# Cosine attention and a highway layer: all short products in two row tiles of TensorE, on four PSUM tiles of two banks

## The chip, the cores and the metric

One NeuronCore of a Trainium2 chip runs the whole program. The time is that of one execution on the device in microseconds (us); a smaller number is better. Five engines have instruction streams of their own, each in order: TensorE (PE; its weight loads are shown as PEld), VectorE (DVE), ScalarE (ACT), GpSimd (POOL) and SyncE (SP, which here issues DMAs only). They wait for each other through semaphores.

## The reference

The inputs are q, k and v of 8 batches x 12 heads x 448 rows x 64, two 768 x 768 weights and a bias.

```python
q_n = q / (np.linalg.norm(q, axis=-1, keepdims=True) + 1e-06)
k_n = k / (np.linalg.norm(k, axis=-1, keepdims=True) + 1e-06)
scores = np.matmul(q_n, k_n.transpose(0, 1, 3, 2)) / tau
scores = scores - np.max(scores, axis=-1, keepdims=True)
attn = np.exp(scores)
attn = attn / (np.sum(attn, axis=-1, keepdims=True) + 1e-09)
attn_out = np.matmul(attn, v)
x = attn_out.transpose(0, 2, 1, 3).reshape(B * S, H * D)
H = np.maximum(x @ w_h, 0.0)
T = 1.0 / (1.0 + np.exp(-(x @ w_t + b_t)))
out = T * H + (1.0 - T) * x
```

## The kernel before

**Tiling.** Heads are worked in pairs: step s = 6 b + p is pair p of batch b, 48 steps in all. The two heads of a pair have 64 dimensions each, so a block of 128 partitions holds both. Of the 448 rows of a head, 384 are the main rows (three chunks of 128) and 64 the tail. A batch's output rows go through the highway layer in four groups i (g = 4 b + i): three of 128 x 768, and the 64 tail rows as the fourth, laid out as 128 x 384.

**One step.** `scaled` normalises q and k (L254). `turn` brings them to [dimension, row], by seven TensorE transposes of 128 x 128 and a copy (L577, L580, L257) in batches 0 to 3, and by a DMA in batches 4 to 7. `scores` multiplies three chunks of keys with all queries of both heads, each head in its row tile of 64 (L637, "qk"), and ACT takes the exponential (L643). The key tails of both heads come in one full-array product (L652, "qkt") with its own exponential (L656). `attend` multiplies the exponentials with v, which has a column of ones for the sums: three parts of seven matmuls (L685 with the key tails of both heads in one, L689) and one of eight for the query tails (L705), all full array with 65 moving columns, 130 in L685. DVE takes the reciprocal of the sums (L713) and writes x (L715).

**The highway layer.** `ffn` turns x, by TensorE in batches 0 and 7 (L757), else by DMA, and multiplies it with w_t and w_h (L793). These products run in two row tiles of 64 already. Two row tiles must not write one PSUM bank at once, so each tile takes one half of the columns in one bank; in part 1 they swap banks, after a wait for part 0 to end (L786). The group of tail rows uses two column tiles (L777). ACT takes tanh (L816, L817), DVE the rectified product and the gate (L830, L835, L838), DVE or POOL the last sum (L844), SP stores (L850, L854).

**PSUM.** Three tiles of two banks ("pS", ring S) hold the scores and the highway products; two tiles of one bank ("pB", ring B) hold turned blocks, tail scores and attention sums. A tail group's two products share one pS tile.

**Norms.** The inverse norms of batch 0 are exp(-0.5 ln(n)) on ACT; those of the others are seven DVE operations per group (L460 to L466). The Tanh table holds no Ln, so ACT loads tables twice in all.

**Order.** The program is first recorded as operations, each with its engine, then replayed in the order that the tuple `ORDER` gives; `SLOTS` gives the buffer of each new tile, `MOVED` the operations that go to the second of two possible engines, and `URGENT` which POOL operations DVE has to wait for. No scheduler changes that afterwards. The start, where POOL issues the first loads (L345, L371), is in the same list.

```python
    plan = pl.follow(ORDER, SLOTS)
```

Of the kernel before, what the change touches and what calls it, by code (L numbers as in the profile page):

```python
# [8 lines left out]
FP32 = mybir.dt.float32  # L9
# [161 lines left out]
def kernel(  # L171
# [11 lines left out]
    nc = tc.nc  # L183
# [4 lines left out]
    MH = DM // 2  # L188
    NCH = 3
    inv_tau = 1.0 / float(tau)  # L190
    BY_DMA = (4, 5, 6, 7)
    assert (B, NH, S, D) == (8, 12, 448, 64)

    sb = ctx.enter_context(tc.tile_pool(name="sb", bufs=1))
# [771 lines left out]
```

## Time and profile before

| | |
|---|---|
| median of 3 runs | 274.05 us (273.81 to 274.11) |
| profiled execution | 269.76 us, of which the span of instructions is 268.0 us |
| busy, share of the span | PE 91%, DVE 82%, ACT 77%, POOL 43% |
| granted TensorE clock, mean | 0.967 |
| mean rate of the DMAs | 161 GB/s |
| most time by group | ACT L643 exponentials, 144 x 924 ns; PE L793 highway products, 1152 x 323 ns |

A row of a group gives line, engine, operation, what it writes and reads, the count, then busy time in us and the mean of one in ns, then the engine's idle time before these operations and what ended it. A row of instructions in order of time begins with the start and the duration in us. Matmuls are pipelined: the duration of one holds its latency, and the next starts long before it ends, so that what a matmul costs is read from the starts. A row of stretches gives the busy time of each engine between two times, then the granted clock of TensorE, the share of the DMA engines and their rate.

### The profile page before, as it was taken

What the parts mean: (1) busy time and instruction counts of PE and PEld (TensorE: products, weight loads), DVE (VectorE), ACT (ScalarE), POOL (GpSimd) and SP (SyncE); (2) the same over time, 40 slices, a digit from 0 to 9 for tenths busy, and PEclk for the clock granted to TensorE, in tenths of its full rate; (3) what the DMA queues carried; (4) which work ended last, traced back from release to release, by engine and by line L of the source; (5) the groups of instructions that cost most, each with busy time, mean ns of one, the idle gap of its engine ahead of it and who ended that gap; (6) DMA issues with size and microseconds to landing.
All of it is one profiled execution on the core that took longest, in us unless ns stands there. A gap on an engine that the chain in (4) does not pass through costs nothing.

```text
span 268.0 us, 9080 instructions
## 1 busy us (share of the span) xinstructions
PE 243.8 (91%) x3783; PEld 164.3 (61%) x3783; DVE 220.0 (82%) x501; ACT 206.1 (77%) x279; POOL 116.2 (43%) x150
## 2 busy tenths in 40 slices
PE   6088987899999999999999998999999999999990
PEld 2043665667776667666766775766567757777650
DVE  6598999999999989997999988999877953556483
ACT  3378999789999989989788898969778897671210
POOL 8757359455554567335551535226132501141200
PEclk9567999999999999999999999999999999999996
DMA  7999999999969696999889999999757837123143
GB/s 131 210 192 183 178 199 210 196 183 193 149 97 224 145 172 65 192 213 199 206 136 155 186 244 162 193 137 224 173 115 214 134 63 177 59 92 120 32 181 101
DMA packets 103738, 43.14 MB, mean 161 GB/s; under 512 B 97552, under 2 KB 100624, under 8 KB 103696
## 3 DMA queue, kind: packets, MB, share of 16 engines
q0 software_dynamic: 38464, 16.32, 49.1%
q1 hardware_dynamic: 64000, 25.80, 47.4%
q8 instruction: 30, 0.49, 0.7%
q10 hardware_dynamic: 1232, 0.43, 0.7%
q14 instruction: 12, 0.10, 0.1%
HBM read 37.82 MB, written 11.01 MB: 182 GB/s over the span
## 4 chain that ended last, share of the span: by engine, by line
PE 64%; DVE 17%; DMA 8%; issue 4%; ACT 2%; POOL 2%; SPq 1%; DVEq 0%; POOLq 0%; ACTq 0%
PE pS L793 27%; PE pS L637 8%; PE pB L689 7%; PE pS L777 6%; DMA qT<-qn 6%; PE pB L652 4%; PE pB L705 3%; PE pB L685 3%; PE pB L577 3%; DMA qr<-in_q_dram 2%; DVE os L844 2%; DVE x L715 2%; DVE f L416 2%; PE pB L306 1%; DVE kb L254 1%
## 5 line engine op out<-in xcount | busy, mean ns | idle before, releaser
L643 ACT ACTIVATE E<-pS 128x896 f16<-128x896 f32 x144 | 127.4, 924 | 23.1 <-PE pS L637 21.9
L793 PEld LDWEIGHTS <-xT 64*128 64x128 f16 x1152 | 54.5, 94 | 31.2 <-issue 1.3
L793 PE MATMUL pS<-wh,xT 64*128 64x384 f16 x576 | 58.0, 323 | 0.0
L793 PE MATMUL pS<-wt,xT 64*128 64x384 f16 x576 | 57.1, 323 | 0.0
L637 PE MATMUL pS<-qT 64*128 64x384 f16 x288 | 43.5, 331 | 1.8 <-DMA qT<-qn 1.0
L689 PE MATMUL pB<-vp,E 128*128 128x65 f16 x864 | 43.3, 194 | 0.0
L830 DVE SCALAR_TENSOR_TENSOR hm<-pS,x 128x768 f16<-128x768 f32 (+1 forms) x33 | 27.3, 834 | 17.5 <-PE pS L793 6.9
L689 PEld LDWEIGHTS <-E 128*128 128x128 f16 x864 | 38.5, 98 | 0.7 <-issue 0.6
L637 PEld LDWEIGHTS <-qT 64*128 64x128 f16 x576 | 22.7, 95 | 19.5 <-issue 4.6
L254 POOL TENSOR_TENSOR qn<-kr,rs 128x384 f16<-128x384 f16 x24 | 19.8, 828 | 32.5 <-issue 10.0
L685 PE MATMUL pB<-vp,Et 128*128 128x130 f16 x144 | 31.9, 222 | 0.5 <-DVE vp L257 0.4
L844 POOL TENSOR_TENSOR os<-x,hm 128x768 f32<-128x768 f16 (+1 forms) x11 | 16.7, 1516 | 34.6 <-DVE hm L838 16.4
L817 ACT ACTIVATE tt<-pS 128x768 f16<-128x768 f32 x24 | 19.6, 821 | 14.4 <-PE pS L793 14.3
L715 DVE SCALAR_TENSOR_TENSOR x<-pB,rd 128x448 f16<-128x448 f32 x48 | 29.8, 622 | 1.1
L656 ACT ACTIVATE Et<-pB 128x512 f16<-128x512 f32 x48 | 29.1, 610 | 1.7 <-PE pB L652 1.5
L637 PE MATMUL pS<-tT,qT 64*128 64x64 f16 x282 | 27.6, 190 | 0.0
L705 PE MATMUL pB<-vp,E 128*128 128x65 f16 x288 | 18.4, 194 | 0.6 <-DVE x L715 0.6
L254 POOL TENSOR_TENSOR qn<-qr,rs 128x384 f16<-128x384 f16 x17 | 14.4, 853 | 9.0 <-DVE os L844 3.5
L844 DVE TENSOR_TENSOR os<-x,hm 128x768 f32<-128x768 f16 (+1 forms) x21 | 17.6, 836 | 0.2
L685 PEld LDWEIGHTS <-Et 128*128 128x128 f16 x144 | 14.0, 97 | 5.6 <-issue 4.1
L254 DVE TENSOR_TENSOR qn<-qr,rs 128x384 f16<-128x384 f16 x30 | 16.8, 566 | 0.5 <-POOL qn L254 0.4
L713 DVE RECIPROCAL rd<-pB 128x7 f32<-128x7 f32 x48 | 9.4, 199 | 8.4 <-PE pB L705 4.0
(110 smaller groups left out, 437.4 us busy)
## 6 DMA issues: line engine op xcount, KB each, us to landing
out_dram<-os SPq DMA_DIRECT2D x24, 384.0 KB, 3.2
vr<-in_v_dram POOLq DMA_DIRECT2D x8, 576.0 KB, 11.7
kr<-in_k_dram POOLq DMA_DIRECT2D x7, 576.0 KB, 9.9
qr<-in_q_dram POOLq DMA_DIRECT2D x7, 576.0 KB, 10.2
qt<-in_q_dram SPq DMA_DIRECT2D x16, 96.0 KB, 5.2
vt<-in_v_dram SPq DMA_DIRECT2D x16, 96.0 KB, 5.2
out_dram<-os SPq DMA_DIRECT2D x16, 96.0 KB, 2.3
kt<-in_k_dram SPq DMA_DIRECT2D x14, 96.0 KB, 6.0
```

What stands on the lines that cost most here:

```text
L254: return (nc.vector if eng == "DVE" else nc.gpsimd).tensor_mul(out_, a, c)
L637: ins = nc.tensor.matmul(dst, lhsT=qT[ln, 384 + 128 * c : 512 + 128 * c], rhs=rhs, start=True, stop=True)
L643: return nc.scalar.activation(R("E", s)[:, c, :, 0:448], R("S", 3 * s + c)[:, :, 0:448], AF.Exp, scale=inv_tau)
L656: op("ACT", f"expt {s}", lambda: nc.scalar.activation(R("Et", s)[:, 64:576], R("B", ("S", s))[:, :], AF.Exp, scale=inv_tau), key + 3, r=[( ...
L685: nc.tensor.matmul(U[:, 2 * c : 2 * c + 2, :].rearrange("p g e -> p (g e)"), lhsT=Et[:, 128 + 128 * c : 256 + 128 * c], rhs=vp[:, 6:8, :]. ...
L689: ins = nc.tensor.matmul(U[:, 2 * c + ab, :], lhsT=EF[:, j, 576 * ab + 128 * c : 576 * ab + 128 * c + 128], rhs=vp[:, 3 * ab + j, :], star ...
L705: ins = nc.tensor.matmul(U[:, 6, :], lhsT=lt, rhs=rh, start=(n == 0), stop=(n == 7))
L715: op("DVE", f"ev {s}", lambda: nc.vector.scalar_tensor_tensor(out=R("x", b)[:, :, D * p : D * p + D], in0=U_()[:, :, 0:D], scalar=0.0, in1 ...
L793: ins = nc.tensor.matmul(P[:, h, 0:MH], lhsT=lt, rhs=rh, start=(part == 0 and cc == (-1 if wi == 0 else 0)), stop=(part == 1 and cc == CC ...
L817: return nc.scalar.activation(T.rearrange("p (h m) -> p h m", h=2), P[:, :, 0:MH], AF.Tanh, scale=0.5)
L830: return nc.vector.scalar_tensor_tensor(out=o_, in0=i0, scalar=0.0, in1=xs, op0=ALU.max, op1=ALU.subtract)
L844: op(en, f"out{wd} {g}", lambda: eng.tensor_add(R("os", g)[:, 0:W], xall(), R("hm", g)[:, 0:W]), at + 0.1, r=[("gg", g), ("x", b)], w=[("o ...
```

## The change

Ring B goes; ring S has four tiles of two banks, and everything that TensorE writes goes through it. A tail group of the highway layer takes one tile for each of its products.

Everything that used the full array but the 20 pieces of filling work at the start (`warm`) is split over two row tiles of 64, which write two different banks. A turn of a block is two transposes of 64 columns side by side, whose result is put together again by the copy's access pattern. The tail scores become three parts: each row tile holds one head's keys and takes half of the queries per bank; the banks are swapped after the first part and swapped back for the third. They have an exponential for the main queries and one for the tails. The attention products become four parts of seven matmuls per row tile, 56 a pair in place of 29; each row tile sums over one half of the rows of v, first into the blocks of one bank, then, after a wait, into those of the other. v's tails get one row block per pair with zeros around it in place of two.

The inverse norms of batches 1 and 2 are taken by ACT too (`LOGS`), with the first tanh held until they are done. One square of batch 2 goes to ACT or POOL. The very last tail group takes its gate as (x + 0.5 h) + tanh x 0.5 h, so that only two DVE operations follow the tanh, and its two stores go out on SP and ACT.

`ORDER`, `SLOTS`, `MOVED` and `URGENT` are new. In the new order POOL issues the loads of the first rows of k and q ahead of the bias.

```diff
--- before.py
+++ after.py
...
     BY_DMA = (4, 5, 6, 7)
+    LOGS = 2
...
-              qT=3, tT=2, E=3, Et=3, rd=2, x=3, xT=2, tt=3, hm=3, os=4, S=3, B=2)
+              qT=3, tT=2, E=3, Et=3, rd=2, x=3, xT=2, tt=3, hm=3, os=4, S=4)
...
         S=ring("pS", NR["S"], [128, 2, 512], FP32, ps),
-        B=ring("pB", NR["B"], [128, 512], FP32, ps),
...
+    def half(r):
+
+        return slice(64 * r, 64 * r + 64)
+
+    def flat(i):
+        return R("S", i).rearrange("p k c -> p (k c)")
+
     def R16(i):
-        return R("B", i).bitcast(FP16)
-
-
+
+        return flat(i).bitcast(FP16).rearrange("p (k c) -> p k c", k=2)
+
+    def to_turn(T, at, block):
+
+        for r in range(2):
+            ins = nc.tensor.transpose(T[:, r, 64 * at : 64 * at + 64], block[half(r)], ident[half(r), half(r)])
+        return ins
+
+    def turned(T, lo, n):
+        return T[:, :, 64 * lo : 64 * (lo + n)].rearrange("p r (n l) -> p n r l", l=64)
+
+    def in_blocks(a):
+        return a.rearrange("p n (r l) -> p n r l", l=64)
...
-            eng = pick(eng, "DVE" if eng == "ACT" else "POOL" if b == 1 else "ACT")
+            eng = "ACT" if b == 2 and t else eng
+            eng = pick(eng, "POOL" if b in (1, 2) else "DVE" if eng == "ACT" else "ACT")
...
-        if name[0] == "0":
+        if int(name[0]) <= LOGS:
...
-                at = 128 * (c + 1 - z)
-                nc.tensor.transpose(T[:, at : at + 128],
-                                    R("qn", s // 2)[:, z, c // NCH, c % NCH].rearrange("l ab d -> l (ab d)"), ident[:, :])
+                to_turn(T, c + 1 - z, R("qn", s // 2)[:, z, c // NCH, c % NCH].rearrange("l ab d -> l (ab d)"))
...
             kt_ = kb0[:, :, :] if s == 0 else R("kb", b)[:, p]
-            return nc.tensor.transpose(T[:, 768 * z : 768 * z + 128], kt_.rearrange("l ab d -> l (ab d)"), ident[:, :])
-
-        op("PE", f"turn {s}", fn, key, mode="F",
-           r=[("qn", s // 2, s % 2), ("kb0", 0) if s == 0 else ("kb", b, 0), ("id", 0)], w=[("B", ("T", ti))])
+            return to_turn(T, 6 * z, kt_.rearrange("l ab d -> l (ab d)"))
+
+        op("PE", f"turn {s}", fn, key, mode="T",
+           r=[("qn", s // 2, s % 2), ("kb0", 0) if s == 0 else ("kb", b, 0), ("id", 0)], w=[("S", ("T", ti))])
...
+    swap = {}
+
+    def after(ins, on):
+        tc.add_manual_dep(ins.ins, on.ins.name, mybir.DependencyInfo(
+            mybir.DependencyClass.Sync, mybir.DependencyReason.SCHED_ONLY), reason="order of engines")
+
+    def swapped(name, part):
+
+        if part == 0:
+            return None
+        held = nc.tensor.nop()
+        after(held, swap[name])
+        return held
+
+    def hold(ins, held, r):
+        if held is not None:
+            after(ins, held)
+        return None if r else held
...
-        def ft():
-            S_ = R("B", ("S", s))
+        def ft(part):
+
+            S_ = R("S", ("Q", s))
             qT = R("qT", s // 2)[:, 1 + 6 * z : 4 + 6 * z].rearrange("p c l -> p (c l)")
             keys = R("tT", b)[:, p] if b in BY_DMA else R("qT", s // 2)[:, 13 * z]
-            for dst, rhs in ((S_[:, 0:64], tails()), (S_[:, 64:448], qT), (S_[:, 448:512], tails())):
-                ins = nc.tensor.matmul(dst, lhsT=keys, rhs=rhs, start=True, stop=True)
+            held = swapped(("Q", s), part)
+            for i in ((0,), (0, 1), (1,))[part]:
+                for r in range(2):
+                    h, ln = r ^ (part % 2), half(r)
+                    dst, rhs = ((S_[:, h, 32:224], qT[ln, 192 * h : 192 * h + 192]),
+                                (S_[:, h, 0:32], tails()[ln, 32 * h : 32 * h + 32]))[i]
+                    ins = nc.tensor.matmul(dst, lhsT=keys[ln], rhs=rhs, start=(part == i), stop=(part == i + 1))
+                    held = hold(ins, held, r)
+            swap["Q", s] = ins
             return ins
 
-        op("PE", f"qkt {s}", ft, key + 3, mode="F", r=tok, w=[("B", ("S", s))])
-        op("ACT", f"expt {s}", lambda: nc.scalar.activation(
-            R("Et", s)[:, 64:576], R("B", ("S", s))[:, :], AF.Exp, scale=inv_tau), key + 3,
-           r=[("B", ("S", s))], w=[("Et", s)])
+        for part in range(3):
+            op("PE", f"qkt {s} {part}", lambda part=part: ft(part), key + 3 + 0.1 * part, mode="T",
+               r=tok + [("Q0", s, n) for n in range(part)], w=[("S", ("Q", s))] + [("Q0", s, part)])
+
+        def et():
+
+            for at, lo, n in ((64, 0, 32), (192, 32, 192)):
+                ins = nc.scalar.activation(R("Et", s)[:, at : at + 2 * n].rearrange("p (h q) -> p h q", h=2),
+                                           R("S", ("Q", s))[:, :, lo : lo + n], AF.Exp, scale=inv_tau)
+            return ins
+
+        op("ACT", f"expt {s}", et, key + 3, r=[("S", ("Q", s))], w=[("Et", s)])
...
+        def terms(r, g):
+
+            ln, got = half(r), []
+            EF, Et = R("E", s).rearrange("l c ab q -> l c (ab q)"), R("Et", s)
+            abs_ = range(2) if g == 6 else (g % 2,)
+            if r in abs_:
+                q0 = 64 - 64 * r if g == 6 else 192 + 64 * (g - r)
+                got.append((g, Et[ln, q0 : q0 + 128], 6 * NP + 1 + 4 * p))
+            for ab in abs_:
                 for j in range(NCH):
+                    q0 = 384 + 64 * ab if g == 6 else 576 * ab + 64 * (g - ab)
+                    got.append((g, EF[ln, j, q0 : q0 + 128], 6 * p + 3 * ab + j))
+            return got
+
+        def part_of(n):
+
+
+            part, lot = n // 2, n % 2
+            held, U = swapped(("U", s), part) if lot == 0 else None, U_()
+            todo = [[x for g in (((0, 1), (2, 3)), ((5, 4), (6,)))[r ^ part][lot] for x in terms(r, g)] for r in range(2)]
+            assert len(todo[0]) == len(todo[1])
+            for k in range(len(todo[0])):
+                for r in range(2):
+                    g, lt, at = todo[r][k]
+                    dst, rhs = U[:, g, :], R("vp", b)[half(r), at, :]
+                    first = n == k == 0
+                    if first:
+                        w = slice(0, 4) if r == 0 else slice(4, 7)
+                        dst = U[:, w, :].rearrange("p g e -> p (g e)")
+                        rhs = R("vp", b)[half(r), at - r : at + (4, 2)[r], :].rearrange("l g e -> l (g e)")
+                    ins = nc.tensor.matmul(dst, lhsT=lt, rhs=rhs, start=first, stop=(n == 3 and k == len(todo[r]) - 1))
+                    held = hold(ins, held, r)
+            if n == 1:
+                swap["U", s] = ins
             return ins
...
-        for c in range(NCH):
-            op("PE", f"av {s} {c}", lambda c=c: full(c), key + 0.3 * c, mode="F", r=rd, w=[("B", ("U", s))])
-        op("PE", f"avt {s}", tail, key + 1, mode="F", r=rd, w=[("B", ("U", s))])
+        for n in range(4):
+            op("PE", f"av {s} {n}", lambda n=n: part_of(n), key + 0.3 * n, mode="T",
+               r=rd + [("U0", s, m) for m in range(n)], w=[("S", ("U", s)), ("U0", s, n)])
...
+        def finish_last():
+
+            k_ = key + 5
+            op("DVE", f"ac {g}", lambda: nc.vector.scalar_tensor_tensor(
+                out=R("os", g)[:, 0:W], in0=R("hm", g)[:, 0:W], scalar=0.5, in1=R("x", b)[:, 6, :], op0=ALU.mult, op1=ALU.add),
+               k_, r=[("hm", g), ("x", b)], w=[("ac", g)], u=[("hm", g), ("os", g)], port=True)
+            op("DVE", f"hh {g}", lambda: nc.vector.tensor_scalar_mul(R("hm", g)[:, 0:W], R("hm", g)[:, 0:W], 0.5),
+               k_, r=[("hm", g), ("ac", g)], w=[("hh", g)], u=[("hm", g)], port=True)
+            op("DVE", f"ggh {g}", lambda: nc.vector.tensor_mul(R("tt", g)[:, 0:W], R("tt", g)[:, 0:W], R("hm", g)[:, 0:W]),
+               k_, r=[("tt", g), ("hh", g)], w=[("gg", g)], u=[("tt", g), ("hm", g)], port=True)
+            op("DVE", f"outh {g}", lambda: nc.vector.tensor_add(R("os", g)[:, 0:W], R("os", g)[:, 0:W], R("tt", g)[:, 0:W]),
+               k_, r=[("gg", g), ("ac", g)], w=[("os", g)], u=[("tt", g)], port=True)
+            store_tails((("SP", nc.sync), ("ACT", nc.scalar)))
...
-                op("ACT", f"th{1 if tail else 2} {g}", tanh, at, r=[("Pd", g, 0)], w=[("tt", g)], u=[bank])
+                logs = [("rn", n, p) for n in range(LOGS + 1) for p in range(1 if n == 0 else 0, 7)] if g == 0 else []
+                op("ACT", f"th{1 if tail else 2} {g}", tanh, at, r=[("Pd", g, 0)] + logs, w=[("tt", g)], u=[bank])
```

More of the change, by code (lines that the diff above doesn't have):

```diff
@@ L670, in vtcast @@
     def vtcast(b, key):
-        for ab in range(2):
-            eng = pick("DVE", "POOL")
-            op(eng, f"vtc {b} {ab}", lambda ab=ab, eng=eng: copied(
-                eng, R("vp", b)[64 * ab : 64 * ab + 64, :, 6 + ab, 0:D], R("vt", b)[64 * ab : 64 * ab + 64, :, :]),
-               key, r=[("vt", b), ("zvp", min(b, 1))], w=[("vp", b, 6)], port=eng != "ACT")
+        eng = pick("DVE", "POOL")
+        op(eng, f"vtc {b}", lambda: copied(eng, v_tails(R("vp", b))[:, :, 0:D], R("vt", b)[:, :, :]),
+           key, r=[("vt", b), ("zvp", min(b, 1))], w=[("vp", b, 6)], port=eng != "ACT")
     def attend(b, p, key):
@@ L737, in ffn @@
         last_ = b == B - 1 and i == 2
+        last_tail = b == B - 1 and tail
         nb = 3 if tail else 6
@@ L794, in mm @@
                                                stop=(part == 1 and cc == CC - 1))
-                        if held is not None:
-                            after(ins, held)
-                            held = None if r else held
+                        held = hold(ins, held, r)
                 swap[g, wi] = ins
@@ L840, in ffn @@
            r=[("gt", g), ("hm", g)], w=[("gg", g)], u=[("tt", g), ("hm", g)], port=True)
-        last = b == B - 1 and i >= 2
-        en = "DVE" if last else pick("POOL", "DVE")
+        en = pick("POOL", "DVE")
         eng = nc.vector if en == "DVE" else nc.gpsimd
```

136 lines of the change are left out of this document (56 added, 80 removed), and 152 rows, old and new, of tables (MOVED, ORDER).

## The prediction

> **What bounds the kernel now.** I read the page's parts 1 and 2 first, then a table of stretches, then the instructions of TensorE in order of time, and at last the two ends of the chain of waits.
>
> ```profile
> PE 243.8 (91%) x3783; PEld 164.3 (61%) x3783; DVE 220.0 (82%) x501; ACT 206.1 (77%) x279; POOL 116.2 (43%) x150
> ```
>
> The stretches end where attention of batch 3 and of batch 6 is done (the 24th and the 42nd write of x at L715).
>
> ```profile
> core 0: us, PE busy (x) PEld busy (x) DVE busy (x) ACT busy (x) POOL busy (x), PEclk, DMA share, GB/s
> 0.00:30.00 30.00, 18.66 (x159) 9.98 (x159) 23.55 (x63) 18.48 (x28) 20.59 (x38) 0.77 1.33 180
> 30.00:130.50 100.50, 96.66 (x1615) 68.09 (x1613) 94.04 (x217) 94.13 (x126) 55.46 (x68) 1.00 1.16 174
> 130.50:217.90 87.40, 85.42 (x1382) 57.44 (x1378) 76.67 (x170) 71.82 (x99) 32.23 (x40) 1.00 0.99 169
> 217.90:268.00 50.10, 43.09 (x639) 28.78 (x635) 25.78 (x55) 21.66 (x29) 7.91 (x6) 0.96 0.37 110
> ```
>
> After the start TensorE is nearly always busy: 96.7 of 100.5 us, then 85.4 of 87.4. But in the first of these two stages DVE and ACT are also at 94%; in the second they have 11 and 16 us to spare. So less work for TensorE is worth its full size in the later stages and at most about 6 us in the first. And busy is not the same as at its peak, as its instructions show:
>
> ```profile
> 120.95 0.21 PE L637 MATMUL pS<-tT,qT 64*128 64x64 f16 x2
> 121.09 0.20 PE L652 MATMUL pB<-tT,qT 128*128 128x64 f16 x1
> ...
> 121.82 0.25 PE L705 MATMUL pB<-vp,E 128*128 128x65 f16 x3
> ...
> 122.07 0.22 PE L685 MATMUL pB<-vp,Et 128*128 128x130 f16 x1
> 122.13 0.35 PE L689 MATMUL pB<-vp,E 128*128 128x65 f16 x6
> 122.32 0.19 PE L652 MATMUL pB<-tT,qT 128*128 128x64 f16 x1
> 122.35 0.32 PE L652 MATMUL pB<-qT 128*128 128x384 f16 x1
> 122.51 0.19 PE L652 MATMUL pB<-tT,qT 128*128 128x64 f16 x1
> 122.64 0.34 PE L637 MATMUL pS<-qT 64*128 64x384 f16 x2
> 122.81 0.19 PE L637 MATMUL pS<-tT,qT 64*128 64x64 f16 x2
> 122.84 0.33 PE L637 MATMUL pS<-qT 64*128 64x384 f16 x2
> ```
>
> Count by starts, since a duration holds the latency too. A 64-column step costs 0.03 us, whether it is one full-array matmul (122.32 to 122.35) or two in row tiles (122.81 to 122.84). From the full array to row tiles (122.51 to 122.64) and back (120.95 to 121.09) the same step takes 0.13 and 0.14: a change of mode costs 0.10 us.
>
> **The change, part by part.** I cost the work by starts from these rows and count instructions along the order of each program.
>
> Modes. TensorE changes between full array, row tiles and column tiles 135 times before and 40 times after (56 of the 95 fewer lie in the stages up to batch 3, 29 in the next, 10 behind). 95 x 0.10 = -9.5 us.
>
> Turns. Seven 128-column turns take 0.40 us:
>
> ```profile
> 96.41 0.51 PE L577 MATMUL pB<-ident,qn 128*128 128x128 f16 x6
> 96.75 0.22 PE L580 MATMUL pB<-ident,kb 128*128 128x128 f16 x1
> 96.81 0.50 PE L577 MATMUL pB<-ident,qn 128*128 128x128 f16 x6
> ```
>
> that is 0.057 each. Afterwards a block is two 64-column turns side by side, one 64-column step, 0.03. 221 blocks x 0.028 = -6.2 us, nearly all before batch 4.
>
> Attention products. One part with the key tails takes 0.25 us (122.07 to 122.32), the query tails the same for eight (121.82 to 122.07), so a 65-column step is 0.032 and a pair 1.02 (three parts of 0.254, and 0.26). Afterwards there are 56 half-height matmuls in 28 pairs: 27 x 0.0325 and a first one of 260 columns, 0.11, together 0.99. That is -1.5 us over 48. It assumes that the two of a pair overlap as at 122.81; no row has a long run of short row-tile matmuls, so the ends are 0.03 and 0.065 (one behind the other) a step. I take the first, since the row is the same shape but one column. Scores of key tails: 0.22 before (122.32 to 122.51 and a step), and 0.08 + 0.08 + 2 x 0.03 after: nothing.
>
> The Trainium skill, "TensorEngine Tiling (Array Packing)", Performance Considerations, speaks against this part: each matmul has some 60 cycles of overhead, so one should not tile where a dimension is small already. By the 25 ns that "TensorE: Matmul & The Clock Gate", Back-to-back issue gap, gives for that, 56 matmuls would take an estimated 1.40 us and the sum would come out some 20 us higher. The pair at 122.81 starts its successor after 0.03 us, so this trace does not bear it out for row tiles.
>
> Swaps. Where the row tiles exchange banks, a wait (L786) holds the sequencer until the part before has ended. There are 144 new ones: two per pair in the tail scores, one in the products.
>
> ```profile
> L786 PEldq EVENT_SEMAPHORE  x48: 51/51/51, 48.7 to 256.8; - x48
> ```
>
> The 48 of before cost nothing, since at least 0.19 us of other work lies between. The price is the end of the last matmul (0.19 after its start for 65 columns, about 0.24 for 192), 0.05 for the wait, and by my estimate 0.05 before and 0.03 behind it, since the waits of before all had slack; less the step itself: 0.28 us, less the other work that the order puts between. In the new order 52 of the 144 have less than that, most of them 0.19 and ten of them none: together +6.9 us (4.8, 1.3 and 0.8 by stage).
>
> PSUM. Before, 200 uses shared three tiles of two banks and 153 two of one bank; after, 361 uses share four. Readers hold a tile as long as these rows say:
>
> ```profile
> L643 ACT ACTIVATE E<-pS 128x896 f16<-128x896 f32 x144 | 127.4, 924 | 23.1 <-PE pS L637 21.9
> L830 DVE SCALAR_TENSOR_TENSOR hm<-pS,x 128x768 f16<-128x768 f32 (+1 forms) x33 | 27.3, 834 | 17.5 <-PE pS L793 6.9
> L656 ACT ACTIVATE Et<-pB 128x512 f16<-128x512 f32 x48 | 29.1, 610 | 1.7 <-PE pB L652 1.5
> L715 DVE SCALAR_TENSOR_TENSOR x<-pB,rd 128x448 f16<-128x448 f32 x48 | 29.8, 622 | 1.1
> ```
>
> I laid TensorE's costs along each order and asked at every hand-over if the work between a tile's last matmul and its next first one covers 0.3 us and the reader. Past the first 20 us of TensorE's work, before falls short at 7 of 296, by 2.2 us in all; after at 71 of 298, by 19.0 us (11.9, 5.6, 1.5 by stage). One wait of TensorE pushes back the next use of all four tiles, so these do not add up: at the least a quarter, 4.8 us, at the most 19. I take the quarter, since the swaps' stalls help as well.
>
> So TensorE by stage: -11.5 + 4.8 + 3.0 = -3.7; -3.7 + 1.3 + 1.4 = -1.0; -1.8 + 0.8 + 0.4 = -0.6.
>
> ACT and DVE. The tail's exponential becomes two; from 0.610 for 512 columns and 0.494 for 384 (next fence) 64 columns take 0.2, so +0.08 each, +4 in all; three Ln/Exp pairs for batches 1 and 2, about 0.6 each, +1.8; in return three squares of 1.18 fewer, and one smaller one and two copies of q and k, some 0.9 each: ACT +0 to +1. DVE loses 21 Newton steps (L460 to L466, 0.2 to 0.26 each) and six half casts of v's tails (0.5), and takes on squares and products: some -5, about 2 of it in the second stretch. So that stretch can't go below 94 us of ACT; one slice of 20 us in it has ACT busy for 19.94, so at 97% it ends at 97, a gain of 3.5. I take -3.5 there in place of -3.7.
>
> ```profile
> L816 ACT ACTIVATE tt<-pS 128x384 f16<-128x384 f32 x8 | 4.0, 494 | 6.4 <-PE pS L777 4.1 <-DVE hm L830 2.3
> L260 ACT ACTIVATE sq<-kr 128x1152 f16<-128x1152 f16 x9 | 10.5, 1179 | 0.2 <-DMA qr<-in_q_dram 0.2
> L449 ACT ACTIVATE rs<-n,tiny 128x36 f32<-128x36 f32 x2 | 0.7, 338 | 0.8 <-DVE n L422 0.8
> 60.00:80.00 20.00, 19.87 (x350) 14.43 (x345) 18.86 (x38) 19.94 (x26) 11.08 (x13) 1.00 1.04 147
> ```
>
> Start. The first squares wait for q's rows, which POOL issues behind a bias load that waits for a clear:
>
> ```profile
> 4.90 0.52 POOL bth L371
> 5.42 0.73 POOL qr L345
> 6.15 5.67 DMA qr<-in_q_dram
> 11.90 0.85 ACT sq L260
> 12.78 0.76 DVE f L416
> ```
>
> The new order issues those four loads first: 2 to 3 us earlier. But the first pair's normalising now stands behind their folds (L416, 0.76) on DVE, and more loads are in flight at once. -1.5, between -3 and 0.
>
> End. The last tanh waits for DVE, which reads the same tile:
>
> ```profile
> 261.03 0.56 DVE L830 SCALAR_TENSOR_TENSOR hm<-pS,x 128x384 f16<-128x384 f32 x1 [0.39 <-PE pS L777]
> 261.50 0.95 DVE L844 TENSOR_TENSOR os<-x,hm 128x768 f32<-128x768 f16 x1
> 261.68 0.49 ACT L816 ACTIVATE tt<-pS 128x384 f16<-128x384 f32 x1 [2.02 <-DVE hm L830]
> 263.64 1.11 SPq L850 DMA_DIRECT2D out_dram<-os  x2
> ```
>
> Afterwards it is a tile of its own and the two stores go out on two queues: -1.0 and -0.5 at best; but DVE has the 0.95 of L844 and some 0.6 of new operations to do meanwhile. -0.7, between -0.2 and -1.2.
>
> Sum: -3.5 - 1.0 - 0.6 - 1.5 - 0.7 = -7.3. The profiled execution took 269.76 (span 268.0), so 262.4 for it; the median of the runs stands 4.3 higher, 274.05, and so comes to 266.7.
>
> **Rivals.** First, ACT and DVE decide up to batch 3: each waits for the other often enough that the stage gains 1 us and the start nothing. 274.05 - 1.0 - 1.6 - 0.7 = 270.7. For it: three engines at 94% or more; against: the slice where ACT is full.
>
> Second, slower: four PSUM tiles are too few, and each short hand-over is paid alone. With a share s of the 19 us paid, the change is -17.2 + 6.9 + 19 s - 2.2, so it loses from s = 0.66; at 0.85 it is +3.7, 278. For it: the cover was near 1 us at the median before and is 0.2 to 0.3 now; against: before, TensorE hardly waits for PSUM, and one wait serves four tiles.
>
> Third, slower as well: row-tile matmuls of 65 columns don't overlap in long runs. 56 x 0.0325 - 1.02 = 0.80 a pair, +38.5 in place of -1.5: about 305.
>
> Fourth, the change does not free TensorE at all, since other waits take up all it saves: 274.
>
> **How the numbers follow.** Forecast (262 to 269.5) 0.50; ACT and DVE 0.20; PSUM 0.17; no overlap 0.05; no change 0.03; better than 262, with no hand-over paid and the start at its best, 0.05. Within 0.2% is about what a measurement can't tell from no change. Faster: 0.50 + 0.20 + 0.05 = 0.75; same 0.03; slower 0.22. The range leaves out the fast end, no overlap and the worst of PSUM: 261.5 to 278; the forecast alone has 262 to 269.5.
>
> **What would show it.** Right: 65-column pairs starting every 0.033 us; few 0.10 us steps; new idle of TensorE of 5 to 12 us with ACT E and DVE x as releasers; the end of batch 3 at about 125.5, of batch 6 at 212. Wrong: pairs at 0.065; TensorE's gaps over 17 us; ACT busy under 90% in the first stage with TensorE waiting for it.

## The result and the profile after

The changed kernel takes 306.42 us (median of four runs, 302.94 to 308.92), the kernel before in the same session 273.93: a ratio of 1.1229, 95% interval 1.0962 to 1.1496. The forecast was 266.7. (Where runs of one kernel lie more than 1.5% above its fastest they count as slow: they are left out of ratios and intervals, but not of the medians given here.) The profiled execution took 305.67, span 303.9. From the page of the kernel after (part 1, queues, chain):

```profile
PE 249.1 (82%) x5541; PEld 173.0 (57%) x5541; DVE 215.6 (71%) x473; ACT 204.9 (67%) x328; POOL 118.4 (39%) x153
...
q8 instruction: 44, 0.72, 0.9%
...
PE 68%; issue 11%; DVE 9%; ACT 7%; DMA 3%; POOL 0%; ACTq 0%; PEldq 0%; DVEq 0%; POOLq 0%
```

and the queue's line before:

```profile
q8 instruction: 30, 0.49, 0.7%
```

TensorE's busy time hardly rose (243.8 before), but it fell from 91% of the span to 82%, and 11% of the chain is "issue": time in which the engine waited for nothing that the profile shows. The instructions went from 3,783 matmuls and as many weight loads to 5,541 of each, and the packets of queue 8 from 30 to 44, 16 KB each. The same stretches as before, of the kernel after (stage ends by the 24th and 42nd write of x):

```profile
0.00:30.00 30.00, 15.98 (x243) 8.94 (x243) 22.66 (x59) 17.80 (x30) 22.48 (x38) 1.00 1.30 177
30.00:154.90 124.90, 101.34 (x2498) 72.15 (x2496) 93.66 (x201) 93.87 (x149) 54.83 (x67) 0.93 0.95 144
154.90:252.90 98.00, 88.20 (x1948) 62.09 (x1946) 72.20 (x161) 70.10 (x114) 35.27 (x45) 0.97 0.91 147
252.90:303.90 51.00, 43.54 (x860) 29.80 (x856) 27.10 (x54) 23.08 (x38) 5.79 (x4) 0.99 0.41 111
```

By the start of its last write of x, batch 3 ends at 154.9 and not at 125.5, batch 6 at 252.9 and not at 212. In the second stretch no engine is full any more (TensorE 81%, ACT and DVE 75%), and TensorE's clock is 0.93. What TensorE waited for, in the view of waits:

```profile
PE pS L773 <- issue: 17.6, 12, 3.3
PE pS L334 <- DVE fill L305: 9.7, 1, 9.7
PE pS L874 <- issue: 7.3, 4, 3.2
PE pS L283 <- issue: 2.1, 2, 1.2
PE pS L682 <- ACT E L688: 1.4, 3, 0.7
PE pS L861 <- issue: 1.1, 1, 1.1
```

19 idle times of up to 3.3 us, 28.1 us together, are put down to "issue"; ACT's exponential and DVE's output of attention, which were to be the releasers, are far behind. (The 9.7 us of L334 are the filling work at the start, which waits for a clear.) One of the 19, in TensorE's instructions in order of time:

```profile
90.57 0.36 PE L773 MATMUL pS<-vp,E 64*128 64x65 f16 x12
90.76 0.25 PE L703 MATMUL pS<-qT 64*128 64x192 f16 x2
...
91.53 0.25 PE L773 MATMUL pS<-vp,E 64*128 64x65 f16 x5
95.05 0.23 PE L773 MATMUL pS<-vp,E 64*128 64x65 f16 x1 [3.26 <-issue]
95.17 0.21 PE L703 MATMUL pS<-tT,qT 64*128 64x32 f16 x2
95.22 0.48 PE L874 MATMUL pS<-bth,ones 64*128 64x384 f16 x2
95.50 1.17 PE L874 MATMUL pS<-wt,xT 64*128 64x384 f16 x6
96.45 0.53 PE L874 MATMUL pS<-bth,ones 64*128 64x384 f16 x2
```

TensorE stops in the middle of a run of products whose operands are all there. And this is where it stops: counting the rows of its stream from the first (matmuls, weight loads and the waits that its sequencer executes, 11,282 in all), these stops stand at number 705, 961, 1217, 1729 and so on, 256 rows or a multiple of it apart, and a packet of 256 instructions of 64 bytes has come in 1.2 to 1.7 us before it goes on. For this one the transfers from 92.5 to 94.0 us show the packet, among loads and stores:

```profile
q1 hardware_dynamic: 997, 0.29, 88.6%
q0 software_dynamic: 185, 0.07, 37.4%
q8 instruction: 1, 0.02, 3.9%
```

It came from 92.85 to 93.79. So TensorE had run out of instructions. Counted by starts, 20 of the 42 block boundaries behind 30 us have such a stall, 32.6 us in all; in the kernel before none has. And the long ones cost once more, since the clock (the number behind POOL's count) falls to half; 95.50 to 96.45 above holds three pairs of matmuls, 0.32 each in place of 0.16. Behind 30 us the trace has seven such stretches of 3.4 us at 0.50: after all six stalls of 2 us and more and after one of 1.1, while nine others, of 0.9 to 1.9 us, left the clock at 1.00. Ahead of, in and behind one of the seven:

```profile
88.00:91.50 3.50, 2.96 (x97) 2.20 (x94) 2.47 (x5) 3.34 (x6) 0.25 (x1) 1.00 1.17 144
95.10:97.70 2.60, 2.60 (x19) 1.24 (x21) 0.00 (x0) 1.83 (x5) 0.00 (x0) 0.50 0.25 73
98.00:101.00 3.00, 3.00 (x56) 1.98 (x54) 2.18 (x6) 0.56 (x3) 1.70 (x2) 1.00 0.01 3
```

The Trainium skill, "Runtime: NRT & Kernel Launch", Instruction fetch mechanics, describes blocks of 16 KiB, 256 instructions, fetched by the sequencer on a queue of its own, and calls the cost of crossing a boundary "mostly hidden". This trace agrees with the block (44 packets, stalls 256 rows apart), not with the cost: it is hidden before, and 28.1 us of idle time here.

### The profile page after: what moved, and what is told of

The parts are those of the page before. It is cut to its first block, busy times and chain, and to the rows that moved or that the text cites. A ratio compares the mean times of both kernels' runs of the same rounds, so it can differ in the third digit from the quotient of the medians.

```text
span 303.9 us, 12784 instructions
## 1 busy us (share of the span) xinstructions
PE 249.1 (82%) x5541; PEld 173.0 (57%) x5541; DVE 215.6 (71%) x473; ACT 204.9 (67%) x328; POOL 118.4 (39%) x153
## 4 chain that ended last, share of the span: by engine, by line
PE 68%; issue 11%; DVE 9%; ACT 7%; DMA 3%; POOL 0%; ACTq 0%; PEldq 0%; DVEq 0%; POOLq 0%
PE pS L874 33%; PE pS L773 15%; PE pS L682 9%; PE pS L861 5%; PE pS L703 4%; ACT E L688 3%; ACT Et L715 2%; DMA first<-in_k_dram 2%; PE pS L283 2%; DMA kt<-in_k_dram 2%; DVE x L785 1%; DVE qn L258 1%; DVE sq L258 1%; DVE qT L261 1%; DVE f L445 1%
## 5 line engine op out<-in xcount | busy, mean ns | idle before, releaser
L773 PE MATMUL pS<-vp,E 64*128 64x65 f16 x2304 | 63.3, 193 | 18.3 <-issue 17.6
L773 PEld LDWEIGHTS <-E 64*128 64x128 f16 x2304 | 54.8, 96 | 21.8 <-issue 16.8
L773 PE MATMUL pS<-vp,Et 64*128 64x65 f16 (+2 forms) x384 | 44.5, 210 | 0.6 <-DVE qT L261 0.3
L715 ACT ACTIVATE Et<-pS 128x64 f16<-128x64 f32 x96 | 29.4, 364 | 18.4 <-PE pS L703 17.9
L783 DVE RECIPROCAL rd<-pS 128x7 f32<-128x7 f32 x48 | 9.7, 202 | 37.6 <-PE pS L773 28.3
L785 DVE SCALAR_TENSOR_TENSOR x<-pS,rd 128x448 f16<-128x448 f32 x48 | 29.7, 623 | 1.3
L773 PEld LDWEIGHTS <-Et 64*128 64x128 f16 x384 | 25.5, 96 | 6.8 <-issue 3.6
L261 POOL COPY vp<-vr 128x384 f16<-128x384 f16 x25 | 12.7, 519 | 30.0 <-DVE f L445 9.0
L258 POOL TENSOR_TENSOR qn<-kr,rs 128x384 f16<-128x384 f16 x18 | 14.8, 829 | 22.8 <-DVE qn L258 9.5
L334 PE MATMUL pS<-fill 128*128 128x384 f16 x40 | 8.9, 372 | 10.4 <-DVE fill L305 9.7
L258 DVE TENSOR_TENSOR qn<-kr,rs 128x384 f16<-128x384 f16 x29 | 17.0, 595 | 0.1
```

The lines of the kernel that those rows point to most:

```text
L258: return (nc.vector if eng == "DVE" else nc.gpsimd).tensor_mul(out_, a, c)
L261: return nc.scalar.copy(out_, a) if eng == "ACT" else (nc.vector if eng == "DVE" else nc.gpsimd).tensor_copy(out_, a)
L715: ins = nc.scalar.activation(R("Et", s)[:, at : at + 2 * n].rearrange("p (h q) -> p h q", h=2), R("S", ("Q", s))[:, :, lo : lo + n], AF.Ex ...
L773: ins = nc.tensor.matmul(dst, lhsT=lt, rhs=rhs, start=first, stop=(n == 3 and k == len(todo[r]) - 1))
L785: op("DVE", f"ev {s}", lambda: nc.vector.scalar_tensor_tensor(out=R("x", b)[:, :, D * p : D * p + D], in0=U_()[:, :, 0:D], scalar=0.0, in1 ...
```

## The experiments

Theory I: TensorE's instructions come too late. Theory P: swaps and the four PSUM tiles cost the time. Theory O: short row-tile matmuls don't overlap. Stalls are counted as above, by starts at a block boundary behind 30 us.

### Fewer rows, more rows, no swaps, fewer loads

Products of 130 columns, 4 in place of 7:

```diff
-            for k in range(len(todo[0])):
+            for k in (0, 1, 3, 5):
...
-                    dst, rhs = U[:, g, :], R("vp", b)[half(r), at, :]
+                    dst = U[:, g0 : g0 + 2, :].rearrange("p g e -> p (g e)")
+                    rhs = R("vp", b)[half(r), a0 : a0 + 2, :].rearrange("l g e -> l (g e)")
```

> The changed kernel, with the attention products of each row tile taken two blocks of v at a time: 4 matmuls of 130 columns (one of 65) in place of 7 of 65 per part and row tile. The columns streamed through the array stay nearly the same (0.21 us a part in place of 0.23), modes, swaps, tiles and order stay as they are, TensorE's instructions fall from 11,084 to 8,780. Left out: the second block of each pair gets weights that are not its own, so the sums are not attention. Theory I (instruction supply: TensorE's instructions come in blocks of 256, one packet of 16 KB each, and a block that arrives late stops the engine for 0.5 to 3.6 us): the 31 us of stalls shrink below 8 us, time 268 to 280. Theory P (four PSUM tiles and swaps): the hand-overs are the same, time 300 to 306 less 3. Theory O (short row-tile matmuls do not overlap): 285 to 290.

The kernel before with products of 384 columns in two:

```diff
-                        ins = nc.tensor.matmul(P[:, h, 0:MH], lhsT=lt, rhs=rh, start=(part == 0 and cc == (-1 if wi == 0 else 0)),
+                            ins = nc.tensor.matmul(P[:, h, z : z + 192], lhsT=lt, rhs=rh,
```

> The kernel before, with each 384-column product of the scores and of the highway layer (not its tails) as two of 192 columns with the same weights. Same array work (0.082 twice in place of 0.162 a step, some +2 us), same modes, tiles and order; TensorE's instructions rise from 7,568 to 10,544. Theory I: stalls with nothing that ended them appear at every few blocks of 256 instructions, 15 to 30 us, time 287 to 305. Theories P and O: 274 to 278, since nothing of PSUM changes and 192 columns are not short.

No swaps in attention products and tail scores:

```diff
-            held = swapped(("Q", s), part)
+            held = None
...
-                    h, ln = r ^ (part % 2), half(r)
+                    h, ln = r, half(r)
...
-            held, U = swapped(("U", s), part) if lot == 0 else None, U_()
+            held, U = None, U_()
```

> The changed kernel without the 144 new swaps: each row tile keeps its own bank in the tail scores and in the attention products, and the waits are gone. Left out: half of the sums go to the wrong blocks and twice to the others; count and size of all matmuls stay. The prediction's price of the swaps is 6.9 us. Theory I: TensorE gains at most that and then runs into the late blocks sooner, so 300 to 306. Theory P, if the swaps make most of the loss: under 285.

Loads of batches 4 to 7 for 16 of 128 rows:

```diff
+            L = 16 if b >= 4 else 128
-            op("POOL", f"ld6 {rname} {b}", lambda: nc.gpsimd.dma_start(R(rname, b)[:, :, :], main_src(src, b)), key,
+            op("POOL", f"ld6 {rname} {b}", lambda: nc.gpsimd.dma_start(R(rname, b)[0:L, :, :], main_src(src, b)[0:L]), key,
```

> The changed kernel, with the loads of q, k and v's main rows of batches 4 to 7 cut to 16 of 128 rows (the rest is what the buffer held), which takes away 4 of 8 batches' traffic on GpSimd's DMA queue. TensorE's instructions are unchanged. Theory I with waiting behind other DMA traffic as the reason why blocks come late: from about 80 us on the packets of instructions start sooner and the stalls there (about 20 us) fall by half or more, time 280 to 296. Theory I with a fixed delay: unchanged, 302 to 306. Theory P: unchanged.

Measured: wide products 284.34 (four runs from 274.94 to 285.77, too far apart for an interval), stalls 6.0 us; split products in the kernel before 277.57, ratio 1.021 (1.0144 to 1.0276), stalls 3.8; no swaps 292.13, 1.0718 (1.0585 to 1.0852), stalls 9.8; fewer loads 287.08, 1.0577 (1.0497 to 1.0658), stalls 14.9. In all three runs of the changed kernel stalls and time are less than the 32.6 and 306.4 of the full one, and one that touches neither products nor swaps, the loads, takes 19 us away. By its time alone the run with wide products comes nearest to theory O (285 to 290) and over theory I's range, whose stalls it has; what rules O out are the starts, 0.032 us a pair (below). The run without swaps missed both ranges, 300 to 306 and under 285: the swaps cost twice their price, since most of the stalls went with them. And the split kernel before has 10,542 matmuls and weight loads, nearly as many as the changed one (11,082), and only an eighth of the stalls: the number alone is not it (theory I as I had put it for that run missed by 10 us). And with the stalls down, TensorE met a transpose that had not landed, in the view of waits of the run with wide products:

```profile
PE pS L879 <- DMA xT<-x: 6.7, 1, 6.7
```

### Is it the loads themselves, and what is left without stalls?

The same cut of loads in the kernel before; wide products and fewer loads together; and these without swaps too (the tail's exponential there at half its scale, as in the last run of the next part).

> The kernel before with the main loads of q, k and v of batches 4 to 7 cut to 16 of 128 rows (the rest of those rows is left as it was): the control of the same cut in the changed kernel, which was worth 19 us there. Theory I (the loads cost the changed kernel time because TensorE's instruction packets wait behind them): the kernel before has no stall at a block of instructions, so 269 to 273, at most 3 us less. Rival L (less traffic helps any such kernel, through waits for data and buffers): 10 to 19 us less, 254 to 263.

> The changed kernel with both cuts that each took stalls away: attention products as 4 matmuls of 130 columns in place of 7 of 65 (part of the products left out), and the loads of batches 4 to 7 cut to 16 rows. TensorE's array has the same work to within 2 us. Theory I: no more than two stalls at blocks of instructions, and with them the wait for a late transpose gone: 266 to 273. Rivals P and O (PSUM hand-overs, swaps or pairs that do not overlap cost the time): 280 or more, since their work is all still there.

> The one above, with the bank swaps of the attention products and of the tail scores left out as well (each row tile keeps one bank; products wrong in kind, equal in number). With the stalls for instructions gone, this prices the swaps by themselves. The forecast's term: 3 to 7 us less than the one above. Rival: the swaps cost only because a hold-up of TensorE empties what was ready for it, and next to nothing here: within 1.5 us of the one above.

Measured: 268.33 (0.9945, 0.9916 to 0.9974), 276.52 (1.0209, 1.0132 to 1.0286) and 268.93 (0.9945, 0.9898 to 0.9993). The cut that is worth 19 us in the changed kernel is worth 1.5 in the one before, which has no stall. Wide products and fewer loads leave 3.3 us of stalls of 32.6, and the time falls by 29.9 from 306.42: about as much as the stalls. (Some 3.5 of it is the wide products' own: by starts a part takes 0.205 us in place of 0.224, 192 times.) It is still 3.5 over the range of theory I; the next step finds it, for without swaps it falls by another 7.6. The waits of TensorE in this last run hold no "issue" any more (the first line is the filling work at the start again):

```profile
PE pS L334 <- DVE fill L305: 9.3, 1, 9.3
PE pS L684 <- ACT E L690: 3.9, 10, 1.1
PE pS L881 <- DMA xT<-x: 2.0, 1, 2.0
PE pS L780 <- ACT E L690: 1.5, 4, 0.4
PE pS L684 <- DVE qT L261: 1.0, 4, 0.3
PE pS L684 <- DVE x L792: 0.9, 2, 0.6
```

So the account of 306.4: some 30 us for the supply of instructions (the half clock, and 3.5 of the wide products, among them) and 7.6 for the swaps with the last 3.3 of stalls, and then the changed kernel is level with its control (268.9 to 268.3), not 14 us below it as the forecast without its swaps would have it (-7.3 - 6.9). With products of 65 columns it would by this estimate stand 3.5 us above.

### What holds a packet up?

First nearly all later traffic was cut from the full changed kernel, then the transposes of q and x of batches 4 to 7 as well, then instead the swaps:

```diff
+        K = 8 if b >= 4 else 64
...
-                R("qT", m)[:, 1 + 6 * z : 7 + 6 * z, :], R("qn", m)[:, z].rearrange("l t c ab d -> l (t c ab d)"),
-                transpose=True), key
+                R("qT", m)[0:16, 1 + 6 * z, :], R("qn", m)[0:16, z].rearrange("l t c ab d -> l (t c ab d)")[:, 0:128]), key
```

> The changed kernel in full on TensorE (11,084 rows, swaps kept), with nearly all of the later DMA traffic cut: loads of batches 4 to 7 to an eighth, key, query and value tails of these too, and all stores to an eighth. Theory I with queueing (a packet of instructions starts late because other transfers are ahead of it): stalls at blocks of instructions are left only before 75 us and come to 5 to 9 us in all, 276 to 284. Rival: a packet starts late for a reason of its own (how fast TensorE eats a block): stalls of 13 us or more, as with the loads alone cut, and 285 or more.

> The run with little traffic (282.8), with the DMA transposes of q and of x of batches 4 to 7 replaced by copies of 4 KB (what they turned is not turned). In that run packets of instructions still start 3 to 6 us after a block's first instruction where a transpose's traffic lies between. Theory I-T (packets wait behind transposes as behind loads): behind 160 us all packets start within 1.6 us, no stall over 0.3 us there, 277 to 281. Rival (something in TensorE's own instructions delays the request, since the same blocks are late in run after run): the same late starts (4.7 us at the block of instruction 6337, 3.2 at 8641), and 282 to 284.

> The run with little traffic (282.8: loads of batches 4 to 7 and all stores cut to an eighth) without the bank swaps of attention products and tail scores, with 10,940 rows on TensorE. Measured from a block's first instruction, packets started 1.9 us later at the median from 150 to 235 us with the swaps' waits and 0.75 in the run without swaps but with all loads. Theory W (the waits on TensorE's queue hold the next request up, traffic adds to it): behind 75 us no packet starts over 3 us late, median under 1.0, stalls left only before 75 us, 272 to 278. Rival (the rate alone: 256 instructions in 2 to 3 us of short products): stalls of 4 us or more behind 75 us, and 279 to 283.

Measured: 282.79 (1.0408, 1.0317 to 1.0499), stalls 15.5; 281.08 (1.031, 1.0257 to 1.0363), stalls 14.6; 274.49 (1.0146, 1.0077 to 1.0215), stalls 7.4, of which 0.3 behind 75 us. The first has its time in the range of theory I but its stalls in the rival's, and the second takes the transposes out as the cause: the blocks at rows 6337 and 8641 still got their packets 4.6 and 3.3 us late. The third was forecast right but for one packet, 4.6 us late at 140 us, which stopped nothing. (Its rows with the sequencer's waits are 11,138, not the 10,940 of the expectation.) How long after a block's first instruction the next packet starts, median from 150 to 235 us of each trace (and how many over 3 us; "FFN only" are the 48 swaps of the highway layer, which every kernel has):

| kernel | loads | swaps | median us | over 3 us |
|---|---|---|---|---|
| before | all | FFN only | 0.74 | 0 of 10 |
| after | all | all | 2.67 | 5 of 13 |
| fewer loads | few | all | 2.04 | 3 of 15 |
| little traffic | few | all | 1.86 | 3 of 15 |
| no transposes | few | all | 1.66 | 3 of 16 |
| no swaps | all | FFN only | 0.75 | 0 of 13 |
| little traffic, no swaps | few | FFN only | 0.48 | 0 of 15 |
| wide products | all | all | 1.1 | 1 of 11 |
| wide, fewer loads | few | all | 1.1 | 0 of 13 |
| wide, fewer loads, no swaps | few | FFN only | 0.5 | 0 of 12 |
| before, split products | all | FFN only | 1.2 | 1 of 14 |

In all three pairs that differ by the swaps, their waits on TensorE's queue make the requests late; traffic adds to it. But how fast rows are used up seems to count as well: with wide products and all swaps the median is 1.1, and the split kernel has 1.2 without one new swap. No one of the three makes the 2.67 alone. Up to 75 us, where the weights come in too, the medians are some 2.7 before and 3 to 4 in the changed kernels of the table, with swaps and without; the transfers of that stretch were not cut, so their part was not tried. A packet takes 0.9 to 1.1 us and TensorE goes on 1.2 to 1.7 later; so a block must last some 2.1 to 2.8 us plus the late start. Blocks last 6.2 to 10.4 us before; after, the products alone use up 4 rows in 0.032 us, and blocks of 2.7 to 5 us come up. In the split kernel before a block has 5.7 at the median and packets start 1.2 to 1.7 late behind 75 us: it just holds.

### Where did TensorE's saving go?

From the run without stalls and swaps on, three pairs of kernels, each the changed one and its control run side by side: squares and folds of q and k for a third of the columns; then also the exponential for 448 of 896 columns; then all other readers of PSUM tiles too.

```diff
-                return nc.scalar.activation(R("E", s)[:, c, :, 0:448], R("S", 3 * s + c)[:, :, 0:448], AF.Exp, scale=inv_tau)
+                hi = 448 if s < 3 else 224
+                return nc.scalar.activation(R("E", s)[:, c, :, 0:hi], R("S", 3 * s + c)[:, :, 0:hi], AF.Exp, scale=inv_tau)
...
-            out=R("x", b)[:, :, D * p : D * p + D], in0=U_()[:, :, 0:D], scalar=0.0,
+            out=R("x", b)[:, 0:m, D * p : D * p + D], in0=U_()[:, 0:m, 0:D], scalar=0.0,
```

> The changed kernel with wide products, fewer loads and no swaps (the run that came out level with the kernel before, 268.9), with ACT's and DVE's work that no PSUM tile waits for cut as well: squares of q and k and their folds from batch 1 on for a third of the columns (norms wrong). By rows of its trace up to the end of batch 3 that takes some 8 us from ACT and 13 from DVE, which stand at 94 and 95% there. Theory A (ACT and DVE set the end of batch 3, and so TensorE's saving of some 17 us buys nothing): batch 3 ends 4 to 9 us earlier, 260 to 265 in all. Rival P (four PSUM tiles are too few whatever the readers' queues hold): 267 to 269.

> The same cut of squares and folds in the kernel before with fewer loads (268.3): the control. There TensorE itself is busy for 96% up to batch 3, so theory A gives at most 3 us less: 265 to 268. If it gains as much as the run above, ACT and DVE bound the kernel before just the same.

> The changed kernel with wide products, fewer loads, no swaps and fewer squares and folds (268.7), and from the fourth pair on the exponential of the scores for 448 of its 896 columns: ACT holds a PSUM tile for some 0.55 us in place of 0.92. Theory P (TensorE's saving of some 17 us is lost at the hand-overs of the four PSUM tiles, that is to how long readers hold them): 10 to 16 us less, 253 to 259, and 6 us or more below the control. Rival (the saving in array steps was never there): no lower than the control, 262 to 267.

> The control: the same cut of the exponential in the kernel before with fewer loads, squares and folds (266.2). TensorE's own steps are its limit, so at most 4 us less by theory P: 262 to 266.

> The changed kernel as in the run with the shorter exponential (262.9), with the other readers of PSUM tiles cut too, DVE's and ACT's: attention's output from batch 3 on for 3 of 7 columns groups, the gates' tanh and the hidden part from batch 2 on for one half of two, the tail's exponential and the copies of turned blocks from batch 1 on for about half (the parts left out keep old values). By rows of that trace a reader then holds a tile for 0.3 to 0.55 us in place of 0.5 to 0.9. Theory P (the saving in array steps is lost at hand-overs, now to DVE's readers): 250 to 257, and 5 us or more below its control. Rival (the array saves nothing): within 3 us of the control.

> The control: the same cuts of all readers in the kernel before with shorter exponential (264.2). Its TensorE waits for few hand-overs, so 0 to 4 us less: 260 to 264.

| | changed, no stalls, no swaps | control | difference |
|---|---|---|---|
| readers as they are | 268.93 | 268.33 | +0.6 |
| fewer squares and folds | 268.67 | 266.21 | +2.5 |
| and a shorter exponential | 262.90 | 264.16 | -1.3 |
| and all readers shorter | 257.92 | 264.04 | -6.1 |

Theory A falls: with this much room the stretch up to batch 3 has no full engine left, and yet batch 3 ended 1.5 us earlier, not 4 to 9, and the total fell by 0.3 us. The first row is of the run as it was, the second with fewer squares and folds (TensorE, weight loads, DVE, ACT as before):

```profile
30.00:130.30 100.30, 91.33 (x1960) 67.75 (x1956) 95.02 (x202) 93.64 (x151) 50.86 (x67) 1.00 0.82 135
```
```profile
30.00:130.30 100.30, 91.97 (x1982) 68.35 (x1976) 85.36 (x204) 88.99 (x153) 49.40 (x67) 1.00 0.84 140
```

For the first three rows the intervals of the two kernels overlap; for the last they lie well apart. The shorter exponential alone gave 5.8, not the 10 to 16 expected; in its trace the waits had gone over to DVE's readers (x, the hidden part, the copies of turned blocks). With these short too the saving shows, 6.1 us below the control (0.9482, 0.9419 to 0.9545, against 0.9728, 0.9673 to 0.9784). That run came out just over the 250 to 257 expected. So TensorE does have less to do, and loses it waiting for readers; some 3.5 of the 6.1 can be the wide products again, so that what the change itself saves here may be no more than 2.6. Counted by starts from 30 to 258 us, steps that a reader of a PSUM tile (exponentials, x, hidden part, tanh, turned blocks) released were 23.3 us longer than their matmuls in the run without stalls and swaps, 5.5 in its control. The count takes in waits for what a reader writes (attention products read the exponentials), not only for its tile; no run tells the two apart.

### The start

In the kernel before, three entries of the order (a bias load, two clears) moved behind the first loads; then also the second of the last two stores issued by ACT.

```diff
-18 17 2 3 5 0 77 20 19 33 82 21 6 23 11 4 83 24 29 22 76 1 16 8 73 86 28 74 41 25 36 80 40 9 42 27 26 35 32 43
-277 44 31 45 275 7 46 30 55 47 48 273
+18 17 2 3 5 77 20 19 33 82 21 6 23 11 4 83 24 29 22 76 1 16 73 86 28 74 41 25 36 80 9 42 27 26 35 32 43
+277 44 31 45 275 7 46 30 0 40 8 55 47 48 273
```

> The kernel before with three entries of the written order (a bias load on POOL and two clears) moved behind the four first loads of q and k for the second pair. The forecast's start term alone: 1.5 us faster, between 0 and 3 (ratio 0.989 to 1.000). Rival: the first pair's chain, not those loads, sets the start: 0.998 to 1.003. Rival: more loads in flight at once delay the first rows: slower by up to 2 us.

> The kernel before with the first loads issued earlier (as tried before: 0.9966) and the second of the two last stores issued by ACT. Start as before 1.7 us at the first output of attention, 1.0 at the end; the store 0.5 at best. 0.992 to 0.998 of the kernel before. If the stores' issue is not on the path: the same 0.9966 as without it.

Measured: 270.86, 0.9966 (0.9911 to 1.002), and 270.83, 0.9936 (0.9888 to 0.9984). In the first trace attention's first output comes at 28.0 us in place of 29.8, the 42nd at 216.3 in place of 217.3: 1.8 us gained, 1.0 kept. Whether the store adds anything can't be told from these intervals. The second kernel leaves nothing out and is 0.6% faster than the kernel before, with an interval that barely stays below 1.

## Why the prediction was wrong

**The sum had no term for the supply of instructions.** The step that failed first is "I cost the work by starts from these rows and count instructions along the order of each program": instructions were counted as steps of the array only. In row tiles a step of 0.032 us is two matmuls and two weight loads, so what I booked as -1.5 us for the products added 48 x 27 matmuls and as many weight loads, 2,592 rows, to TensorE's stream. Part 3 of the page before had the line to see it in (30 packets of 16 KB on queue 8); I did not read it. It cost some 30 us, the half clock after long stalls included. That packets were late was also due to the 144 swaps, which I had priced by their stall alone.

**Modes, turns, products: right.** 40 changes of mode, about 0.095 us each by starts. Turns, in the kernel after:

```profile
89.08 0.34 PE L283 MATMUL pS<-ident,qn 64*128 64x64 f16 x12
89.25 0.19 PE L283 MATMUL pS<-ident,kb 64*128 64x64 f16 x2
```

six pairs in 0.17 us, 0.028 each. Six pairs of 65-column products take 0.19 us (90.57 to 90.76 above), 0.032 each: the third rival did not happen, and that its 305 us lies so near the 306.4 measured is chance. The Trainium skill's rule on tiling small dimensions ("TensorEngine Tiling (Array Packing)", Performance Considerations), cited in the prediction, is not borne out by these rows.

**Swaps: +6.9, measured 7.6** with nearly all stalls out of the way (of which up to 3.3 can be the last stalls, so 4.3 to 7.6), and a larger price with them, 14 us.

**PSUM hand-overs: the mis-sized term.** I took a quarter of 19.0 us, since "one wait serves four tiles" and the swaps would help. With the whole 19.0 the changed kernel without swaps comes to -14.2 + 14.2 = 0 against before; measured +0.6 against the control, or some 4 without the wide products' 3.5. This is the second rival, with its share at about one, or a little over: without stalls the change would still have lost, some 5 us (276.52 less 3.3 of stalls, against 268.33). By stage, the run without stalls and swaps against its control: +1.1 up to batch 3, +3.2 up to batch 6, -0.8 behind; these profiled executions lie 3.5 us apart where the medians differ by 0.6.

**ACT and DVE as the bound (first rival): no.** More room for them alone gave 0.3 us.

**Start: wrong.** Attention's first output comes at 31.2 us after and 29.8 before, +1.4 and not -1.5, although the earlier loads by themselves are worth 1.8 there. The chain of the kernel after shows where the first part of it went:

```profile
1.51 5.33 DMA first<-in_k_dram
6.86 0.48 ACT first_sq L516
7.38 4.63 DMA kt<-in_k_dram
12.03 0.53 ACT sq L264
12.59 0.77 DVE f L445
```

ACT issues the second half of the key tails only after its first square, which waits for the first rows; the tails' own square comes at 12.03, and the fold of 0.77 us starts at 12.59, against 12.78 before. Then the last product of the first pair starts 0.6 us later than before (29.8 against 29.2), and DVE has two squares ahead of the sums' reciprocal and a fold behind it (29.11 to 31.19): the rest of the 1.4 is DVE's queue, not TensorE's. No run changed either.

**End: right.** From the last write of x to the end 24.5 us before, 22.8 after: -1.7, of which I had -0.7 for the end and -0.6 for TensorE.

What stays open: whether hand-overs would be covered with four tiles in another order, how much of the time lost to readers is the tiles and how much the wait for what readers write, and why a wait on TensorE's queue delays the next request.

## What to carry to other kernels

Count an engine's instructions beside its time: a change that halves the time of each instruction doubles the rate at which blocks of 256 are used up, and the profile's instruction queue, set against the time from block to block, tells how far the next packet is from being late. Read "issue" in the waits as a question, and look where in the stream it falls: if every 256 rows, it is the supply. And a saving in the busiest engine's steps is only worth what the readers of its results leave it; shortening all of them in both kernels shows it.

## What the runs showed of the hardware

TensorE stopped for up to 3.6 us between two matmuls that were ready, because the next 256 instructions had not come; the packet is used 1.2 to 1.7 us after it has landed. In the changed kernel's trace the granted clock stood at 0.50 for 3.4 us after all six stops of 2 us and more; of ten stops of 0.9 to 1.9 us one was followed by it. Waits between matmuls on TensorE's queue put the start of the next packet off, from 0.75 to 2.67 us at the median with 65-column products, and from 0.5 to 1.1 with 130. Two 65-column matmuls in row tiles cost 0.032 us together.
